# Linear attention and two MLPs on one core: six resident feature chunks instead of eight, five Strassen pairs instead of four, a fourth kv buffer, and the small elementwise work assigned anew

## The chip, the cores and the metric

The kernel runs on one core of a Trainium2 chip. The metric is the device time of one execution in microseconds. A time of a profiled execution and the span of its trace (first to last instruction) are told apart where both occur. Engines are named as in the profile: PE is TensorE (PEld its weight loads), DVE is VectorE, ACT is ScalarE, POOL is GpSimd, SP is the engine whose queue issues all loads and stores.

## The reference

Random-feature attention of 4 batches x 8 heads x 576 tokens x 64, and two MLPs (512 to 2048 to 512) on its 2304 tokens, all in fp32:

```
def phi(x):
    proj = np.einsum('bhsd,md->bhsm', x, omega)
    sq = np.sum(x * x, axis=-1, keepdims=True) / 2.0
    h = proj - sq
    h = h - np.max(h, axis=-1, keepdims=True)
    return np.exp(h) / np.sqrt(m)
q_p, k_p = (phi(q_s), phi(k_s))
kv = np.einsum('bhsm,bhsd->bhmd', k_p, v)
z = np.sum(k_p, axis=2)
num = np.einsum('bhsm,bhmd->bhsd', q_p, kv)
den = np.einsum('bhsm,bhm->bhs', q_p, z)[..., None] + 1e-06
# x = num / den, heads side by side
h = x @ w_in;  g = h * np.tanh(softplus(h));  x = g @ w_out        # first MLP (Mish)
h = x @ w_in;  g = h * sigmoid(h);            out = g @ w_out      # second MLP (SiLU)
```

## The kernel before

**Split numbers.** A matmul whose operands must keep fp32 accuracy runs as three fp32r matmuls: each operand is split into a high part (a copy rounded to fp32r, on ACT) and a low part (the rest, a subtraction). `mm3` issues high x high, low x high, high x low (lines 203 to 205).

**Attention.** There are 36 K units (batch b, unit j of 9; four heads by 128 tokens) and 36 Q units. A K unit loads `kin` (ring of 3 buffers, 5 for the first seven units), squares k (`ksqr`, one fused instruction a head on DVE, or a product on POOL with a sum on DVE and a scaling on POOL), projects (`kproj`), takes the maximum (`kmax`, DVE, L374), forms the bias in two instructions of 128x4 elements (`kba`, `kbb`, on POOL, L377 and L379), takes exp (ACT, four instructions), and adds its products with v to the batch's accumulator (`kacc`). When a batch's units of a half are done, `k_finish` leaves the split kv and the broadcast sums z in the rings `kv` and `z` (3 buffers each). A Q unit does the same up to exp (its q is split by `qhi` on ACT and `qlo` on POOL), then the denominator `den` (DVE, one fused instruction a head, or a product `fz` on POOL and a reduction on DVE), `dea`, `der` (L537, L538), the normalisation `fn`, the transpose `tr`, the split `hiT`, `loT`, and, for each second unit, the product with kv (`num`), whose result goes into the split block X by `xev` (ACT) and `xlo` (DVE, L595). Two of these, 256 tokens by 512 features, make a block; there are 9, so 18 xlo.

**First MLP beside attention (phase 0).** The weights of NA = 8 of the 16 feature chunks lie split in 16 resident tiles W. As soon as block j is there, 4 steps of two chunks each run on it: h (24 matmuls of 256 columns), Mish, the split `gh` and `gl`, and y (24 matmuls). They fill the PE between the pieces of attention. The partial results go to a scratch tensor.

**The rest (phases 1 to 4).** The other 8 chunks of the first MLP and all 16 of the second are taken in pairs by Strassen on the blocks: 512 tokens by a pair of chunks take 7 products (42 matmuls of 256 columns) and 24 matmuls of 512 columns for y; the single ninth block takes 24 and 24 of 256 columns. Phase 1 has 4 pairs for each of the 5 (double) blocks, phases 2 to 4 the 8 pairs of the second MLP, four at a time. The operands of a pair are made while the pairs before it run (`conv_pair`): load, ACT and three DVE integer instructions a weight tile (`wb`, `wo`, `ws`, lines 614 to 618), sums `sq` on DVE, and high and low parts (`sh` on ACT, `sl` on POOL, L633). They live in units of 512 columns taken from buffers that attention no longer needs: ring vw1 (34 units, 7 a pair) and vw2 (20 units, 4 a pair).

**Order.** All work is entered as tasks with an engine, a cost, a key (the due time, shifted by the table OFF) and its dependencies; `Plan.order` runs through them as a list scheduler with these costs and emits the instructions in the resulting order. Engines run their queues in that order, whatever the true times are. So the tables and costs move instructions on every engine.

Of the kernel before, what the change touches and what calls it, by code (L numbers as in the profile page):

```python
# [27 lines left out]
NA = 8  # L28
# [40 lines left out]
class Plan:  # L69
# [9 lines left out]
    def add(self, name, eng, cost, key, fn, reads=(), writes=(), new=(), after=(), lat=None, tab=None):  # L79
# [19 lines left out]
        self.tasks.append(dict(name=name, eng=eng, cost=cost, key=key, fn=fn, deps=deps, new=list(new), tab=tab,  # L99
# [94 lines left out]
def performer_two_mlps(ctx: ExitStack, tc: tile.TileContext, qin, kin, omT, w1, w2, out):  # L194
# [26 lines left out]
    ring("kv", tags("kv", 3), [P, 2, 4, 192], F32R)  # L221
    ring("z", tags("z", 3), [P, 8, NF], F32)
# [91 lines left out]
    for rg, parts in (("vw1", ((early, 11), (mid, 3), (static, 20))), ("vw2", ((early, 6), (mid, 2), (static, 12))),  # L314
# [33 lines left out]
    def sums(nm, src, sm, r, key, n, load):  # L348
# [6 lines left out]
        if VAR["sq" + nm][n] == "P":  # L355
# [646 lines left out]
```

## Time and profile before

| | |
|---|---|
| time, median of 3 runs | 989.49 us (989.46 to 990.44) |
| the profiled execution | 990.8 us |
| its span | 989.0 us |
| PE busy | 953.7 us (96%) |
| DVE busy | 616.9 us (62%) |
| ACT busy | 523.1 us (53%) |
| POOL busy | 398.7 us (40%) |
| mean granted PE clock | 0.979 of full speed |

The time is the number that the change is judged by; the span and all rows are of the one profiled execution, which is 1.3 us above the median. Matmuls are pipelined, so PE's busy time counts overlapping rows, and an interval in which it is fully busy may hold fewer matmuls than it could.

### The profile page before, as it was taken

The page shows a single profiled execution, that of the slowest core. Times are in us where ns is not written, and L with a number is a line of the kernel's source. Part 1 is how long each engine was busy: PE and PEld are TensorE (multiplying, and loading weights), DVE is VectorE, ACT ScalarE, POOL GpSimd, SP SyncE. Part 2 cuts the span into 40 slices and gives each one's busy share as a digit, 9 for nine tenths or more (in the row PEclk, how much of TensorE's full clock was granted, in tenths as well). Part 3 has the DMA queues.
Part 4 walks back from the last instruction along what each step waited for, and adds up shares of the span by engine and source line. Part 5 has one row for each costly group of instructions (what it writes and reads, how often), then busy time and mean ns, then how long its engine had stood idle before and what let it go on. Part 6 is the DMA issues. An engine that isn't in the chain of part 4 may idle for free.

```text
span 989.0 us, 17895 instructions
## 1 busy us (share of the span) xinstructions
PE 953.7 (96%) x6628; PEld 886.6 (90%) x6628; DVE 616.9 (62%) x1395; ACT 523.1 (53%) x1139; POOL 398.7 (40%) x526
## 2 busy tenths in 40 slices
PE   7888899999999999999999998999999999999998
PEld 6777799999999999898998897788988988988998
DVE  5798787648778376965543879944437864353422
ACT  4696777678878545552433465534336534334321
POOL 4788565254454255650312565704116433032100
PEclk7798899999999999999999999999999999999999
DMA  8566334322322244423232244340212301230202
GB/s 269 192 195 212 99 118 145 107 82 97 97 97 89 73 119 126 162 64 105 92 106 78 89 129 147 121 139 22 85 31 100 117 1 65 66 123 16 86 1 86
DMA packets 50360, 102.56 MB, mean 104 GB/s; under 512 B 4960, under 2 KB 17504, under 8 KB 50272
## 3 DMA queue, kind: packets, MB, share of 16 engines
q1 hardware_dynamic: 50272, 101.41, 31.8%
q8 instruction: 52, 0.85, 0.3%
q14 instruction: 36, 0.29, 0.1%
HBM read 78.85 MB, written 22.54 MB: 103 GB/s over the span
## 4 chain that ended last, share of the span: by engine, by line
PE 86%; DVE 6%; issue 2%; DMA 2%; POOL 2%; ACT 2%; SPq 0%; DVEq 0%; POOLq 0%; ACTq 0%
PE y L203 12%; PE y L204 12%; PE y L205 12%; PE h L203 5%; PE h L205 5%; PE h L204 5%; PE ha L203 4%; PE ha L204 4%; PE ha L205 4%; PE acc L422 4%; PE hb L203 3%; PE hb L204 3%; PE hb L205 3%; PE kpj L411 3%; DMA kin<-in_kin_dram 2%
## 5 line engine op out<-in xcount | busy, mean ns | idle before, releaser
L709 DVE TENSOR_TENSOR gl<-e,gh 128x512 fp32r<-128x512 f32 x144 | 109.2, 767 | 113.6 <-ACT gh L708 113.3
L205 PE MATMUL y<-gl,W 128*128 128x256 f32 (+1 forms) x528 | 170.4, 323 | 1.9 <-DVE gl L709 1.9
L203 PE MATMUL y<-gh,W 128*128 128x256 f32 (+1 forms) x528 | 171.6, 325 | 0.0
L204 PE MATMUL y<-gh,W 128*128 128x256 f32 (+1 forms) x528 | 170.3, 323 | 0.0
L708 ACT CAST gh<-e 128x512 fp32r<-128x512 f32 x144 | 88.1, 622 | 50.8 <-PE y L204 49.4
L205 PEld LDWEIGHTS y<-gl,W 128*128 128x128 f32 x528 | 99.3, 188 | 11.2 <-DVE gl L709 2.5
L203 PEld LDWEIGHTS y<-gh,W 128*128 128x128 f32 x528 | 99.5, 188 | 6.7 <-DVE stg L842 0.2
L204 PEld LDWEIGHTS y<-gh,W 128*128 128x128 f32 x528 | 99.5, 188 | 6.6
L707 ACT ACTIVATE e<-hb 128x512 f32<-128x512 f32 x48 | 28.7, 598 | 129.4 <-DVE hb L760 129.4
L633 POOL TENSOR_TENSOR LX<-Lqin,LX 128x512 fp32r<-128x512 f32 x23 | 31.7, 1380 | 137.1 <-ACT LX L632 107.0
L203 PE MATMUL h<-X,W 128*128 128x256 f32 x288 | 83.9, 291 | 0.4 <-ACT e L707 0.4
L205 PE MATMUL h<-X,W 128*128 128x256 f32 x288 | 81.7, 284 | 0.1
L204 PE MATMUL h<-X,W 128*128 128x256 f32 x288 | 81.7, 284 | 0.0
L760 DVE TENSOR_TENSOR hb<-Lfz,hb 128x256 f32<-128x256 f32 x48 | 20.5, 426 | 77.7 <-PE hb L205 77.5
L612 ACT ACTIVATE wa<-wr 128x512 f32<-128x512 f32 x64 | 42.9, 678 | 38.7 <-DVE wt L618 26.6
L633 POOL TENSOR_TENSOR LX<-Lqf,LX 128x512 fp32r<-128x512 f32 x15 | 20.7, 1385 | 101.2 <-PE ha L204 52.1
L616 DVE SCALAR_TENSOR_TENSOR wt<-wr,wt 128x512 int32<-128x512 int32 x64 | 58.3, 911 | 0.6
L411 PE MATMUL kpj<-cst,kin 128*128 128x256 f32 x144 | 45.0, 448 | 12.0 <-DMA kin<-in_kin_dram 9.7
L203 PEld LDWEIGHTS h<-X,W 128*128 128x128 f32 x288 | 55.2, 192 | 0.8 <-ACT e L707 0.6
L204 PEld LDWEIGHTS h<-X,W 128*128 128x128 f32 x288 | 55.2, 192 | 0.2
L205 PEld LDWEIGHTS h<-X,W 128*128 128x128 f32 x288 | 55.1, 191 | 0.3 <-DVE X L595 0.3
L707 ACT ACTIVATE e<-h 128x512 f32<-128x512 f32 x48 | 28.1, 598 | 47.2 <-PE h L205 47.0
(620 smaller groups left out, 3127.5 us busy)
## 6 DMA issues: line engine op xcount, KB each, us to landing
wr<-in_w_dram SPq DMA_DIRECT2D x64, 512.0 KB, 4.0
kin<-in_kin_dram SPq DMA_DIRECT2D x35, 386.0 KB, 3.5
qin<-in_qin_dram SPq DMA_DIRECT2D x36, 256.0 KB, 2.9
xf<-sx SPq DMA_DIRECT2D x18, 256.0 KB, 2.4
yp<-stg SPq DMA_DIRECT2D x18, 256.0 KB, 2.2
stg<-yp SPq DMA_DIRECT2D x18, 256.0 KB, 6.2
y<-stg SPq DMA_DIRECT2D x18, 256.0 KB, 2.3
Lqf<-y SPq DMA_DIRECT2D x18, 256.0 KB, 4.7
```

Source lines behind the costliest of these rows:

```text
L203: PE.matmul(o, s_hi, m_hi, start=first, stop=False, skip_group_check=True)
L204: PE.matmul(o, s_lo, m_hi, start=False, stop=False, skip_group_check=True)
L205: PE.matmul(o, s_hi, m_lo, start=False, stop=last, skip_group_check=True)
L411: PE.matmul(t[pj][:, jj * 256:(jj + 1) * 256], t[res][:, jj * P:(jj + 1) * P], t["cst"][:, P:P + 256], start=True, stop=True, skip_group_c ...
L422: PE.matmul(a[:, h, :], t[f][r0:r1, h * NF:(h + 1) * NF], v[r0:r1, h, :], start=first and h == 0, stop=last, skip_group_check=True)
L612: T("wm" + c, "ACT", 0.62, key, lambda: ACT.activation(t[wa], t[raw][:, :, 1].bitcast(F32), AF.Copy, scale=2.0 ** -112), reads=[raw], writ ...
L616: T("wo" + c, "DVE", 0.95, key, lambda: DVE.scalar_tensor_tensor(t[wt], t[raw][:, :, 0], 29, t[wt], ALU.logical_shift_right, ALU.bitwise_o ...
L633: T(f"sl{nm}", "Pool", 0.1 + 1.3 * n / DM, key, lambda: POOL.tensor_tensor(lo(), src(), hi().bitcast(F32), ALU.subtract), reads=res + [rh] ...
L707: T(f"X{s}.{x}", "ACT", 0.6, ks, lambda: ACT.activation(t[e], t[h], AFN), reads=res, writes=[e], new=[(e, "e")], tab=tab)
L708: T(f"gh{s}.{x}", "ACT", 0.62, ks, lambda: ACT.copy(t[gh[x]], t[e]), reads=[e], writes=[gh[x]], new=[(gh[x], "ghi")])
L709: T(f"gl{s}.{x}", "DVE", 0.69, ks, lambda: DVE.tensor_tensor(t[gl[x]], t[e], t[gh[x]].bitcast(F32), ALU.subtract), reads=[e, gh[x]], write ...
L760: T(f"{nm}{s}", "DVE", 0.43, ks, lambda: DVE.tensor_tensor(q(o, ox), q(a, ax), q(b, bx), ALU.add), reads=[r for r in (res(a, ax), res(b, b ...
```

## The change

It takes 6 instead of 8 chunks into phase 0 (3 steps a block) and makes a fifth Strassen pair of the two others. K's keys are packed closer (5 units of key a batch instead of 8) with four kv and z buffers. Nearly all K and Q squares, all bias instructions, most of qlo, all of den, most of fn and 8 of the 12 resident weights' low parts run on DVE, 8 of the 27 gl of phase 0 on POOL. The scaling by -1/16 moves into the bias instructions. Two Q units (3 and 7) project without a split. The units of vw1 and vw2 come in another order, with two fresh tiles F (35 and 20 units), and the planner's costs, keys and lead times are new, with a term that stretches DVE tasks while POOL works.

```diff
-NA = 8
+NA = 6
+NP1 = (NFC - NA) // 2
...
-QLEAD = 10.0
-KLEAD = 20.0
+QLEAD = 13.1
+KLEAD = 22.0
+KSPAN = 5
...
-VAR = dict(sqk="PDPPPPPPPPPDPPPPPPPPPPPPDPPPPPDPPPPP",
+VAR = dict(sqk="DDDDDDDDDDPDDDDDDDDDDPDDDDDDPDDDDDDD",
...
-           den="DDDDDDDDDDPPPDDDDPDPDDDPPDDPDDDDDDPP",
-           fn="AAAAPPPPDDDDPPPDDPPPPAAAAAAAAPPPPPPP",
+           den="DDDDDDDDDDDDDDDDDDDDDDDDDDDDDDDDDDDD",
+           fn="DDADDDDDDDDDDDDDDDDDDPDDDDADDDDDDDPD",
+           gl="DDPDPDDDDDDDPDDDDPPPDDDPDDPDPPPDDDPP",
+           qlo="DPPPDDDPPDDDDDPDPDDDDDDDDDDDDDDDDDPP",
+           wl="DDDPDPPPDDDDPDPD",
+           spl="SSS4SSS4SSSSSSSSSSSSSSSSSSSSSSSSSSSS")
...
+            if t["eng"] == "DVE" and t["kind"] in SHARED:
+                slow = SHARED[t["kind"]]
+                end += slow / (1 + slow) * max(0.0, min(t["cost"] * (1 + slow), free.get("Pool", 0.0) - at))
...
-    ring("kv", tags("kv", 3), [P, 2, 4, 192], F32R)
-    ring("z", tags("z", 3), [P, 8, NF], F32)
+    ring("kv", tags("kv", 4), [P, 2, 4, 192], F32R)
+    ring("z", tags("z", 4), [P, 8, NF], F32)
...
-    for rg, parts in (("vw1", ((early, 11), (mid, 3), (static, 20))), ("vw2", ((early, 6), (mid, 2), (static, 12))),
+    for rg, parts in (("vw1", ((early, 11), (fresh, 3), (mid, 5), (static, 16))), ("vw2", ((early, 6), (fresh, 1), (mid, 5), (static, 8))),
...
-                DVE.scalar_tensor_tensor(x, x, -1.0 / 16, x, ALU.mult, ALU.mult, accum_out=sm[:, r, 0, h:h + 1])
+                DVE.scalar_tensor_tensor(x, x, 1.0, x, ALU.mult, ALU.mult, accum_out=sm[:, r, 0, h:h + 1])
...
-        T(f"{nm}ba{n}", "Pool", 0.4, key, lambda: POOL.tensor_tensor(sm[:, r, 2, :], sm[:, r, 0, :], sm[:, r, 1, :], ALU.add),
+        T(f"{nm}ba{n}", "DVE", 0.09, key, lambda: DVE.scalar_tensor_tensor(sm[:, r, 2, :], sm[:, r, 0, :], -1.0 / 16, sm[:, r, 1, :], ALU.mult,
...
-        key = 8 * b + j * 8 / 9 - KLEAD
+        key = KSPAN * (b + j / 9) - KLEAD
...
-            T(f"qproj{n}", "PE", 0.72, key, proj, reads=[f"HL:{r}h", f"HL:{r}l", "om"], writes=[pj],
+            T(f"qproj{n}", "PE", 0.72, key, proj, reads=[f"HL:{r}h", f"HL:{r}l", "om"], writes=[pj], after=[f"tr{n - 3}"] if n >= 3 else [],
...
+    n1 = NP1
     for bi in (0, 1, 4, 2, 3):
-        block(1, bi, range(0, 4))
+        block(1, bi, range(0, n1))
...
-WKEY = (18.0, 25.0, 32.0, 34.0, 48.0, 64.0, 66.0, 68.0, 80.0, 98.0, 100.0, 102.0)
-XLEAD = 5.0
+W1, W2, W3 = (-20.0, -13.2, -4.4, -1.5, 1.3), (-3.4, 0.0, 1.5, 8.6), (-6.2, 0.8, 4.4, 6.5)
+XLEAD = 2.1
```

Where the order moves, two places. The first is DVE's queue early in the K work (smk holds the K units' small sums and biases, kpj a projection, kin a K unit's input, wt and W a weight on its way). Before, around the sixth projection:

```order
L357 TENSOR_REDUCE smk<-kin_245 128x4
L374 TENSOR_REDUCE smk<-kpj_279 128x4
L614 TENSOR_SCALAR wt_1_0_305<-wr_1_0_183 128x512
L449 TENSOR_TENSOR kv_135<-acc_0_216,kv_135 128x2x2x64
L616 SCALAR_TENSOR_TENSOR wt_1_0_305<-wr_1_0_183,wt_1_0_305 128x512
L357 TENSOR_REDUCE smk<-kin_261 128x4
L374 TENSOR_REDUCE smk<-kpj_315 128x4
L618 SCALAR_TENSOR_TENSOR wt_1_0_305<-wa_1_0_247,wt_1_0_305 128x512
```

And after, around the same projection:

```order
L389 TENSOR_REDUCE smk<-kpj_271 128x4
L643 TENSOR_TENSOR W_87<-wt_0_0_214,W_87 128x512
L382 SCALAR_TENSOR_TENSOR kin_267,smk<-kin_267 128x64 x4
L464 TENSOR_TENSOR kv_133<-acc_0_222,kv_133 128x2x2x64
L392 SCALAR_TENSOR_TENSOR smk<-smk 128x4
L382 SCALAR_TENSOR_TENSOR kin_281,smk<-kin_281 128x64 x4
L389 TENSOR_REDUCE smk<-kpj_305 128x4
L394 SCALAR_TENSOR_TENSOR smk<-smk 128x4
L389 TENSOR_REDUCE smk<-kpj_326 128x4
L392 SCALAR_TENSOR_TENSOR smk<-smk 128x4 x2
```

The squares (four fused rows a unit, L382), the biases (L392, L394) and the low part of a resident weight (L643) now stand in DVE's queue; the reductions of POOL's squares (L357) are gone from it.

The second is the PE's queue shortly before the fifth num (the number in kin, kpj and kf is the K unit, in acc the batch and half, in qpj and tp the Q unit, in h and y the step). Before:

```order
L205 MATMUL h5_1562<-X1_1127,W20_91 128x256
L411 MATMUL kpj25_1583<-cst_119,kin25_1371 128x256 x2
L422 MATMUL acc2_1_1337<-kin24_1329,kf24_1549 128x65 x4
L554 MATMUL tp9_1602<-cst_119,qf9_1489 128x128 x4
L203 MATMUL qpj11_1616<-om_127,HL_109 128x256
L204 MATMUL qpj11_1616<-om_127,HL_109 128x256
L205 MATMUL qpj11_1616<-om_127,HL_109 128x256
```

After:

```order
L217 MATMUL h4_1669<-X1_1087,W30_93 128x256
L437 MATMUL acc3_0_1525<-kin30_1554,kf30_1710 128x65 x4
L426 MATMUL kpj32_1744<-cst_117,kin32_1612 128x256 x2
L437 MATMUL acc3_0_1525<-kin31_1575,kf31_1734 128x65 x4
L437 MATMUL acc3_1_1764<-kin31_1575,kf31_1734 128x65 x4
L472 MATMUL zt3_0_1776<-cst_117,zb3_0_1769 128x128 x4
L215 MATMUL y0_0_1_1440<-gh2_0_1648,W41_96 128x256
```

At the same place of attention the K work has come to the units of the last batch (32 of 36), where before it was in the third (25); the Q work and the steps of phase 0 stand about where they stood.

## Rows read from the trace of the kernel before

**Rows 1.** Page, sections 1 and 2: PE's busy time, and its share in 40 slices.

```profile
PE 953.7 (96%) x6628; PEld 886.6 (90%) x6628; DVE 616.9 (62%) x1395; ACT 523.1 (53%) x1139; POOL 398.7 (40%) x526
...
PE   7888899999999999999999998999999999999998
```

**Rows 2.** Timeline of PE: start us, length, engine, line, tiles, shape, count.

```profile
179.24 1.89 PE L411 MATMUL kpj<-cst,kin 128*128 128x256 f32 x8
180.77 0.47 PE L203 MATMUL qpj<-om,HL 128*128 128x256 f32 x1
...
395.23 0.28 PE L203 MATMUL y<-gh,W 128*128 128x256 f32 x1
...
820.26 0.28 PE L203 MATMUL hb<-LX,W 128*128 128x256 f32 x1
...
823.12 0.40 PE L203 MATMUL y<-gh,Lz 128*128 128x512 f32 x1
...
825.89 0.28 PE L203 MATMUL ha<-LHL,Lkv 128*128 128x256 f32 x1
```

**Rows 3.** The first xlo (all of L595), the fifth xlo, phase 1's first matmul.

```profile
L595 DVE TENSOR_TENSOR X<-xp,X x18: 676/690/692, 63.8 to 347.0; 128x512 fp32r<-128x512 f32 x18
...
146.63 0.68 DVE L595 TENSOR_TENSOR X<-xp,X 128x512 fp32r<-128x512 f32 x1
...
396.29 0.28 PE L203 MATMUL hb<-LHL,Lkf 128*128 128x256 f32 x1
```

**Rows 4.** Windows: stretch, PE, PEld, DVE, ACT, POOL busy, PEclk, DMA, GB/s.

```profile
0.00:64.50 64.50, 51.79 (x258) 44.60 (x258) 45.53 (x131) 40.23 (x118) 43.64 (x95) 0.81 0.69 223
64.50:147.30 82.80, 73.13 (x512) 68.40 (x512) 66.48 (x199) 61.13 (x151) 56.45 (x103) 0.90 0.49 151
147.30:396.30 249.00, 246.81 (x2071) 244.89 (x2070) 169.05 (x507) 174.36 (x399) 109.85 (x173) 1.00 0.33 103
396.30:989.00 592.70, 581.96 (x3794) 528.75 (x3792) 335.81 (x561) 247.42 (x474) 188.75 (x158) 1.00 0.26 84
```

**Rows 5.** Waits, 64.5 to 147.3 us: total us, times, longest.

```profile
DVE FT L563 <- ACT FT L562: 4.2, 3, 3.1
...
SPq L405 <- PE acc L422: 31.1, 10, 11.5
```

**Rows 6.** Tiles gl and sq on DVE: length ns min/median/max, first and last start.

```profile
L709 DVE TENSOR_TENSOR gl<-e,gh x144: 674/691/1785, 108.1 to 981.5; 128x512 fp32r<-128x512 f32 x144
...
L651 DVE TENSOR_TENSOR sq<-sq,wt x12: 407/412/1499, 264.8 to 798.8; 128x256 f32<-128x256 f32 x12
```

**Rows 7.** Timeline of DVE at three places: start us, length.

```profile
137.37 0.69 DVE L374 TENSOR_REDUCE smk<-kpj 128x4 f32<-128x512 f32 x1
137.98 0.22 DVE L367 SCALAR_TENSOR_TENSOR qin<-qin 128x64 f32<-128x64 f32 x1
138.12 0.08 DVE L367 DVE_READ_ACCUMULATOR qin<-qin 128x1 f32 x1
...
160.42 0.28 DVE L529 SCALAR_TENSOR_TENSOR fz<-qf,z 128x128 f32<-128x128 f32 x1
160.63 0.08 DVE L529 DVE_READ_ACCUMULATOR fz<-qf,z 128x1 f32 x1
...
171.03 0.17 DVE L537 TENSOR_SCALAR smq<-smq 128x4 f32<-128x4 f32 x1
171.23 0.18 DVE L538 RECIPROCAL smq<-smq 128x4 f32<-128x4 f32 x1
```

**Rows 8.** Groups on POOL, 0 to 147.3 us: busy us, mean ns, idle before.

```profile
L627 POOL TENSOR_TENSOR W<-wt,W 128x512 fp32r<-128x512 f32 x16 | 21.3, 1332 | 6.9 <-ACT W L626 6.5
L356 POOL TENSOR_TENSOR kin<-kin 128x256 f32<-128x256 f32 x25 | 16.6, 664 | 8.7 <-DMA kin<-in_kin_dram 8.1 <-issue 0.2
```

**Rows 9.** Windows from 600 us on, columns as in rows 4.

```profile
600.00:625.00 25.00, 21.62 (x144) 19.40 (x143) 24.99 (x41) 13.75 (x27) 17.15 (x14) 1.00 0.43 146
...
600.00:650.00 50.00, 44.18 (x269) 38.53 (x268) 44.70 (x69) 28.90 (x58) 29.70 (x25) 1.00 0.38 126
```

More of the change, by code (lines that the diff above doesn't have):

```diff
@@ L54 @@
 TABLE = 1.3
+SHARED = dict(wb0=0.8, wo0=0.5, ws0=0.4, wl0=0.5, wb1=0.8, wo1=0.5, ws1=0.4, gl=0.5, ksqr=0.75, qsqr=0.75, den=0.75, fn=0.5,
+              qlo=0.5, xtbx=1.2, sa=1.2, kba=1.5, kbb=1.5, qba=1.5, qbb=1.5, dea=1.5)
 def kind_of(name):
@@ L98, in add @@
             self.users.setdefault(x, []).append(i)
-        self.tasks.append(dict(name=name, eng=eng, cost=cost, key=key, fn=fn, deps=deps, new=list(new), tab=tab,
+        self.tasks.append(dict(name=name, eng=eng, cost=cost, key=key, fn=fn, deps=deps, new=list(new), tab=tab, kind=kind_of(name)[0],
                                lat=LAT.get(eng, 0.0) if lat is None else lat))
@@ L532, in q_unit @@
         if den_d:
-            T(f"den{n}", "DVE", 1.7 * len(segs), key, den, reads=[f] + [f"z{b}:{g}" for b, _, _ in segs],
+            T(f"den{n}", "DVE", 0.68 * len(segs), key, den, reads=[f] + [f"z{b}:{g}" for b, _, _ in segs],
               writes=[fz, f"smq:{r}d"], new=[(fz, "fz")])
@@ L676, in performer_two_mlps @@
         for f in range(0, NA, 2):
-            steps.append(dict(ph=0, bi=j, js=[j], N=256, fs=[f, f + 1], first=f == 0, last=f == NA - 2, key=4 * j + f / 2))
+            steps.append(dict(ph=0, bi=j, js=[j], N=256, fs=[f, f + 1], first=f == 0, last=f == NA - 2, key=4 * j + 4.0 * f / NA))
     at, firsts = 4.0 * NBLK, {}
@@ L687, in block @@
             firsts["at"] += w
+    n1 = NP1
     for bi in (0, 1, 4, 2, 3):
-        block(1, bi, range(0, 4))
+        block(1, bi, range(0, n1))
     for bi in (0, 1, 4, 2):
-        block(2, bi, range(4, 8))
-    block(3, 3, range(4, 12))
+        block(2, bi, range(n1, n1 + 4))
+    block(3, 3, range(n1, n1 + 8))
     for bi in (2, 1, 0, 4):
-        block(4, bi, range(8, 12))
+        block(4, bi, range(n1 + 4, n1 + 8))
+    a0, a1, a3 = 4 * NBLK, firsts[1, 3][1], firsts[3, 3][1]
+    WKEY = [a0 + x for x in W1[:n1]] + [a1 + x for x in W2] + [a3 + x for x in W3]
     END = firsts["at"]
@@ L708, in act @@
             T(f"gh{s}.{x}", "ACT", 0.62, ks, lambda: ACT.copy(t[gh[x]], t[e]), reads=[e], writes=[gh[x]], new=[(gh[x], "ghi")])
-            T(f"gl{s}.{x}", "DVE", 0.69, ks, lambda: DVE.tensor_tensor(t[gl[x]], t[e], t[gh[x]].bitcast(F32), ALU.subtract),
+            low = "P" if ph == 0 and VAR["gl"][s] == "P" else "D"
+            T(f"gl{s}.{x}", dict(D="DVE", P="Pool")[low], dict(D=0.69, P=1.4)[low], ks, lambda: dict(D=DVE, P=POOL)[low].tensor_tensor(
+                t[gl[x]], t[e], t[gh[x]].bitcast(F32), ALU.subtract),
               reads=[e, gh[x]], writes=[gl[x]], new=[(gl[x], "glo")])
```

57 lines of the change are left out of this document (29 added, 28 removed), and 3 rows, old and new, of the table OFF.

## The prediction

> **What bounds the kernel now.** I read the page's busy times first: TensorE (PE) is busy 953.7 of 989.0 us, and its slices are below nine tenths in the first eighth, hardly elsewhere [rows 1]. A busy PE says little about its pace, so I took the pace from start to start in the timeline of two undisturbed stretches: 24 matmuls of 256 columns take 2.86 us (0.119 each), 12 of 512 take 2.77 (0.231), and nine of phase 0 take 1.06 from 395.23 to 396.29 (0.118) [rows 2, 3]. Two K units' projections take 1.53, 0.8 for one [rows 2]. Then I cut the span in four stages and asked in which of them the PE's matmuls, at that pace, fill the time. A runs to the end of the first xlo, at 64.5 us; B to the end of the fifth, at 147.3; C to the first matmul of phase 1, at 396.3; D to the end [rows 3, 4].
>
> Counting every matmul of the program's order ahead of these places at its pace (with a K unit's projection, products and transposes an estimated 2 us), the PE has 31 us of work in A, 61 in B, 245 in C and 575 in D. So A loses 33 us and B 22; C loses 4 and D 18. C and D are bound by the PE's work. A and B are not: DVE is busy 66.5 of B's 82.8 us, ACT 61.1, POOL 56.5, the granted clock is 0.90 [rows 4], and DVE's waits there are short, of nine sorts, the longest 4.2 us in all [rows 5]. Only taking PE work out, or making B shorter for the work that it does, can move the end.
>
> **The PE's work.** Nine blocks lose one pair of chunks in phase 0: 9 steps of 48 matmuls at 0.118 is 51.0 us out. A fifth pair by Strassen has, for each of four double blocks, 42 matmuls of 256 columns and 24 of 512, 5.0 + 5.54 = 10.5 us, and 48 x 0.119 = 5.7 us for the single block: 47.9 us in. Two Q units now project in four-pass fp32 instead of six split matmuls, about 0.3 us more (two of the K projections' size). Net: 2.8 us less. That is all that the PE gains; the rest is where it waits.
>
> **DVE's work, without and with GpSimd.** The old small work went partly to GpSimd, and GpSimd slows DVE. gl, which reads two SBUF tiles, has a minimum of 674 ns, a median of 691 and a maximum of 1785; sq goes from 407 to 1499 [rows 6]. Free of that, DVE's rows lie start to start 0.61 us for 512 elements, 0.146 for one head's squares (0.22 long, the accumulator's read beside the next one), 0.21 for one head of den [rows 7], that is, 0.07 to 0.08 less than their length. With those spacings I counted DVE's order ahead of the fifth xlo. Before: 93 us (38 max 23, 16 weight conversions 25, 36 sums 12, 11 den segments 9, 8 squares 5, the rest 19), and it took 147.3. After: 128 us: 48 squares of four heads at 0.585 make 28, 46 max 28, 12 conversions 18.5 and 8 low parts 5, 14 den segments 12, 92 bias rows of 128x4 at 0.09 8, 11 normalisations and 11 loT 13, 10 qlo 3, the rest 12. Ahead of the first xlo it is 39 before and 46 after. The bias rows have no row on DVE before: the nearest are L537 and L538, 0.17 and 0.18 long, 0.20 apart where one reads the other's result [rows 7]; with other work between them I take their length less 0.08, so 0.09, and keep 0.20 as the upper end.
>
> In return POOL falls nearly silent. Before, up to 147.3 us, it had 16 low parts of weights of 1.33 us, 25 K squares of 0.66 [rows 8], and the scalings, biases and products; by the new order it has 14 tensor operations ahead of the fifth num: four low parts, four qlo, five squares, one gl. I price the contention that is left in B at 3 us (2 to 4 of them collide, at the 0.7 us by which sq and gl stretch on the way to their maxima).
>
> **Stage A.** 7 us more of DVE's spacings, some 8 us less stretching, the same load order in kind (the first rows of the load queue are the K units with the same weights between them). DVE has 19 us idle here. I take no change, 64.5; bounds 62 and 69.
>
> **Stage B.** After: DVE 81 us + 3 of contention, PE 76 us (20 K projections between the first and fifth num where 11 stood). DVE is the longest. At 95% busy this is 89.5 us. I choose 95%, between B's present 80% and the 24.99 of 25 us that DVE reaches where everything waits for it [rows 9]; it is nearer to the second, because DVE is then the longest of the stage and other work stands behind each of its waits. Lower bound 82 (never idle, no contention); upper bound, B's present share of 80%: 84/0.80 = 105. So B is +6.7 us, but it holds 34 K units instead of 26 at its end.
>
> **Stage C.** The PE's work left is 286 - 107 = 179 us, where it was 336 - 92 = 245 in 249. DVE has 123 us up to the eighteenth xlo, over 155 of PE: 79%, where it was 111 over 193. The Q chain has less cover: 24 us of PE work follow the last num, 52 before. I take 7 us of loss instead of 4: C is 186. Bounds: 3 (182) and 20 (199, DVE at 85% with its stretched rows). The rule that qproj stands behind the transposes of three units earlier is an order on the PE alone, no wait. The fourth kv and z buffers cost one memset of half a microsecond on an idle POOL; without them K could not run a whole batch further ahead.
>
> **Stage D.** +47.9 for the pair. The worst stall (PE 21.6 of 25 us from 600, 44.2 of 50) comes when pairs 5 to 7 are converted while phase 2 starts: DVE 44.7 of 50 busy, POOL 29.7 [rows 9]. After, all 35 and 20 units of the weight rings are full with five pairs, so nothing is converted far ahead; but by DVE's order the 13 weights of that transition stand beside 16 gl rows instead of 10 weights beside 10. I take 2 us less: D is 638.6. Bounds 7 less (no stall left) and 8 more (pairs 2 to 4 late at the start of phase 1, or another such stall).
>
> **Sum.** 64.5 + 89.5 + 186 + 638.6 = 978.6 us of span, 10.4 less than the 989.0 of the profiled execution. That execution took 990.8 in all, the median of three runs is 989.49; the same difference gives **979 us**. Low ends together make about 960, high ends 1021.
>
> **A rule that speaks against it.** L537 and L538 show 0.17 and 0.18 us for four elements a partition [rows 7], nearly all of it fixed. [...]
>
> **Rivals.** (1) *DVE becomes the bound and the kernel is slower.* If DVE stays at B's present 80%, or a bias row holds it 0.20 us (56 of them in B, 6 us more) and it stands at 88%, B is 103 to 105; C then begins with DVE late and loses 14: 64.5 + 105 + 193 + 638.6 = 1001, **1002 us**. For it: in B all engines are tied in a web, and POOL now helps with none of it. Against: ACT and POOL hops leave the chain from the squares to exp. It decides from a busy share of DVE below 84% in B, where B is 100 and the gain is gone. (2) *K's buffers set the pace: no change.* kin has three buffers, and the loads already wait 31.1 us in B for the products that free them [rows 5]. 20 K units in 89.5 us leave 13.4 us for load, squares, max, bias, exp and product; the present B takes 3 x 7.5 = 22. At 15 us B is 100, and the time **989 us**: the change only moved K's work. Against: K units waited there because their keys were spread, not because a chain needs 22 us. (3) *More than forecast.* DVE at 98%, C losing 3, D's stall at 600 gone: 63 + 86 + 182 + 635 = 966, **966 us**. For it: the old stretch of gl and wt by GpSimd goes from all of A to C.
>
> **How the numbers follow.** Forecast (970 to 987) 0.44; rival 3 0.20; rival 2 0.13; rival 1 0.23. Two tenths of a per cent, 2 us, is about what a measurement of this kernel can tell from no change. Faster 0.64, same 0.13, slower 0.23. The range reaches to rival 3's middle and near to rival 1's: 964 to 998; the forecast's own is 970 to 987.
>
> **What would show it.** Right: the fifth xlo near 154 us with 34 K units done; DVE over 90% busy between 65 and 154; gl's median and mean alike up to phase 1; PE full from 154 to a first phase 1 matmul near 340; D 638 us. Wrong: the fifth xlo after 165, idle DVE there behind ACT or loads, PE gaps over 15 us between the fifth xlo and phase 1, or new PE waits for pairs 2 to 4 or 5 to 8 in phases 1 and 2.

## The result and the profile after

The changed kernel takes **1004.1 us** (median of four, 999.1 to 1004.7) where the kernel before takes 990.0 beside it: a ratio of 1.0136, 95% interval 1.0105 to 1.0168. Measured again later (e9 below) it was 998.2 (997.1 to 1003.4), ratio 1.0110 (1.0066 to 1.0154). It is 1.1 to 1.4% slower; the prediction was 979 and faster. The profiled execution took 1004.05 us with a span of 1002.3. Executions of this kernel differ by some 6 us even where nothing is changed, and the last section shows where; A and B of one profile are read with that margin. D differs too: it is 651.8 in this profile, and 649.6, 650.7 and 647.8 in three more runs with the same order of work from there on (e9, e2, e1).

The page of the profile after: busy time, and PE's share in 40 slices (cf. [rows 1]).

```profile
PE 962.8 (96%) x6504; PEld 889.5 (89%) x6504; DVE 678.8 (68%) x1989; ACT 516.7 (52%) x1106; POOL 270.8 (27%) x241
...
PE   8877899999999989999999999899999999999998
```

The four stages by windows, as in [rows 4]; they end at the first and fifth xlo and at phase 1's first matmul.

```profile
0.00:65.00 65.00, 54.74 (x253) 46.67 (x254) 48.98 (x280) 34.55 (x102) 6.33 (x14) 0.76 0.62 204
65.00:169.00 104.00, 90.41 (x624) 84.78 (x623) 86.70 (x479) 70.90 (x185) 10.51 (x11) 0.92 0.41 128
169.00:350.50 181.50, 179.90 (x1527) 178.98 (x1526) 160.82 (x618) 137.86 (x302) 45.87 (x43) 1.00 0.36 116
350.50:1002.30 651.80, 637.80 (x4106) 579.06 (x4104) 382.32 (x616) 273.38 (x518) 208.04 (x174) 0.99 0.26 84
```

I counted the PE's rows of each stage at the pace of [rows 2] (0.117 us for 256 columns, 0.232 for 512, 0.216 for each row of a K projection, 0.11 for the small ones). A stage's length less this work is its loss, in us:

| stage | before | forecast | after | loss before | loss after |
|---|---|---|---|---|---|
| A | 64.5 | 64.5 | 65.0 | 29.5 | 30.3 |
| B | 82.8 | 89.5 | 104.0 | 19.5 | 24.3 |
| C | 249.0 | 186 | 181.5 | 5.8 | 4.6 |
| D | 592.7 | 638.6 | 651.8 | 16.6 | 28.1 |

PE's work itself went from 917.65 to 914.97 us, 2.7 less (forecast 2.8 less). So the change lost 16 us: 11.5 in D and 5.6 in A and B, and gained 1.2 in C. B and D are the two steps to explain.

B: what SP and DVE wait for (cf. [rows 5]; total us, times, longest). The K loads now wait 57 us for the products that free the three kin buffers, where it was 31.

```profile
SPq L420 <- PE acc L437: 57.0, 18, 9.2
...
DVE smk L389 <- PE kpj L426: 7.2, 7, 3.0
```

D: the two stretches that hold 17 of its 28 us of loss by the same count. The second lost 7 us before ([rows 9]: PE 44.2 of 50) and loses 9.5 now; the start of phase 1 lost 2 before and loses 8.

```profile
350.00:375.00 25.00, 20.89 (x142) 20.21 (x142) 23.93 (x31) 13.30 (x28) 18.73 (x16) 0.86 0.56 179
...
600.00:650.00 50.00, 44.64 (x262) 39.91 (x262) 42.78 (x65) 24.84 (x47) 25.65 (x22) 0.93 0.30 96
```

DVE hardly rests there, and POOL is busy beside it. What the PE waits for after 345 us is above all DVE (total us, times, longest):

```profile
PE ha L215 <- DVE hb L781: 8.9, 5, 2.7
PE ha L215 <- ACT e L726: 1.8, 1, 1.8
```

The granted clock adds to it. Before, it was 1.00 in all of D [rows 4]; now it is 0.86 and 0.93 in the two stretches above. A mean of 0.86 over 25 us and of 0.93 over 50 says that the PE stood at the lower of its two levels for some 14 us in all, which costs up to 7 us where it had work: an estimate from these two rows. (Windows of 1 us show 1.00 or 0.50, but for those in which the level changes; matmuls of 256 columns begin 0.21 us apart at 356 us, at 0.50, and 0.12 at 351, at 1.00.) In this trace each of the four falls comes within 2 us of the end of a PE gap of 1.8 to 2.7 us. Not every such gap brings one: before, the clock stayed up behind a gap of 3.1 us at 612.

The timeline of DVE and POOL at the start of phase 1, DVE first (start, length):

```profile
349.80 1.67 DVE L633 SCALAR_TENSOR_TENSOR wt<-wa,wt 128x512 int32<-128x512 int32 x1
351.39 1.76 DVE L729 TENSOR_TENSOR gl<-e,gh 128x512 fp32r<-128x512 f32 x1
353.07 1.50 DVE L629 TENSOR_SCALAR wt<-wr 128x512 int32<-128x512 int32 x1
354.61 1.66 DVE L631 SCALAR_TENSOR_TENSOR wt<-wr,wt 128x512 int32<-128x512 int32 x1
356.30 0.69 DVE L633 SCALAR_TENSOR_TENSOR wt<-wa,wt 128x512 int32<-128x512 int32 x1
...
349.18 1.74 POOL L649 TENSOR_TENSOR LHL<-wt,LHL 128x512 fp32r<-128x512 f32 x1
350.88 1.73 POOL L649 TENSOR_TENSOR LX<-Lqin,LX 128x512 fp32r<-128x512 f32 x1
352.75 1.55 POOL L649 TENSOR_TENSOR LHL<-wt,LHL 128x512 fp32r<-128x512 f32 x1
354.25 1.47 POOL L649 TENSOR_TENSOR LX<-Lqin,LX 128x512 fp32r<-128x512 f32 x1
```

The two engines take turns. POOL's first row ends at 350.92, DVE's at 351.47; POOL's second at 352.61, DVE's at 353.15; and so on. A DVE row that takes 0.69 us by itself takes 1.7 when it begins beside a POOL row, and only the last one, with POOL idle, has its own length. POOL's rows are stretched too (the shortest of this kind in the trace take 1.27). L649 is the subtraction that makes the low parts of the pairs' weights and of the inputs. The gl that DVE does in phase 0, on the other hand, are free of this now (length in ns, minimum, median and maximum up to 350 us; the maximum over all was 1785 in [rows 6]):

```profile
L729 DVE TENSOR_TENSOR gl<-e,gh x18: 660/682/693, 127.8 to 343.9; 128x512 fp32r<-128x512 f32 x18
```

### The profile page after: what moved, and what is told of

The parts are those of the page before. It is cut to its first block, busy times and chain, and to the rows that moved or that the text cites. A ratio compares the mean times of both kernels' runs of the same rounds, so it can differ in the third digit from the quotient of the medians.

```text
span 1002.3 us, 17826 instructions
## 1 busy us (share of the span) xinstructions
PE 962.8 (96%) x6504; PEld 889.5 (89%) x6504; DVE 678.8 (68%) x1989; ACT 516.7 (52%) x1106; POOL 270.8 (27%) x241
## 4 chain that ended last, share of the span: by engine, by line
PE 59%; DVE 4%; POOL 2%; issue 1%; ACT 0%; DVEq 0%; POOLq 0%; ACTq 0%
PE y L215 10%; PE y L216 10%; PE y L217 10%; PE ha L215 5%; PE ha L216 5%; PE ha L217 5%; PE hb L216 4%; PE hb L215 3%; PE hb L217 3%; PE h L217 1%; PE h L216 1%; PE h L215 1%; DVE wt L629 1%; DVE gl L729 1%; POOL W L649 1%
## 5 line engine op out<-in xcount | busy, mean ns | idle before, releaser
L729 DVE TENSOR_TENSOR gl<-e,gh 128x512 fp32r<-128x512 f32 x136 | 105.4, 782 | 151.7 <-ACT gh L727 143.9
L215 PE MATMUL y<-gh,W 128*128 128x256 f32 (+1 forms) x376 | 122.8, 326 | 0.0
L216 PE MATMUL y<-gh,W 128*128 128x256 f32 (+1 forms) x376 | 121.3, 323 | 0.0
L217 PE MATMUL y<-gl,W 128*128 128x256 f32 (+1 forms) x376 | 121.1, 322 | 0.0
L217 PEld LDWEIGHTS y<-gl,W 128*128 128x128 f32 x376 | 71.7, 191 | 5.8
L215 PEld LDWEIGHTS y<-gh,W 128*128 128x128 f32 x376 | 72.1, 192 | 4.3
L216 PEld LDWEIGHTS y<-gh,W 128*128 128x128 f32 x376 | 72.1, 192 | 4.2
L215 PE MATMUL h<-X,W 128*128 128x256 f32 x216 | 62.6, 290 | 0.0
L216 PE MATMUL h<-X,W 128*128 128x256 f32 x216 | 60.7, 281 | 0.0
L217 PE MATMUL h<-X,W 128*128 128x256 f32 x216 | 60.7, 281 | 0.0
L631 DVE SCALAR_TENSOR_TENSOR wt<-wr,wt 128x512 int32<-128x512 int32 x64 | 60.0, 938 | 0.4
L437 PEld LDWEIGHTS acc<-kin,kf 128*128 128x128 f32 (+1 forms) x320 | 49.0, 242 | 11.0 <-ACT kf L399 9.3
L437 PE MATMUL acc<-kin,kf 128*128 128x65 f32 (+1 forms) x320 | 50.4, 327 | 7.4 <-ACT kf L399 7.4
L781 DVE TENSOR_TENSOR Lfz<-Lfz,ha 128x256 f32<-128x256 f32 x52 | 21.7, 418 | 50.2 <-PE ha L217 47.9
L633 DVE SCALAR_TENSOR_TENSOR wt<-wa,wt 128x512 int32<-128x512 int32 x64 | 54.0, 849 | 0.4
L649 POOL TENSOR_TENSOR LX<-Lqin,LX 128x512 fp32r<-128x512 f32 x23 | 33.2, 1449 | 64.5 <-ACT LX L648 33.2
L629 DVE TENSOR_SCALAR wt<-wr 128x512 int32<-128x512 int32 x64 | 44.6, 699 | 4.9 <-POOL LFT L649 1.5
```

What stands on the lines that cost most here:

```text
L215: PE.matmul(o, s_hi, m_hi, start=first, stop=False, skip_group_check=True)
L216: PE.matmul(o, s_lo, m_hi, start=False, stop=False, skip_group_check=True)
L217: PE.matmul(o, s_hi, m_lo, start=False, stop=last, skip_group_check=True)
L437: PE.matmul(a[:, h, :], t[f][r0:r1, h * NF:(h + 1) * NF], v[r0:r1, h, :], start=first and h == 0, stop=last, skip_group_check=True)
L629: T("wb" + c, "DVE", 0.43, key, lambda: DVE.tensor_scalar(t[wt], t[raw][:, :, 1], -0x80000000, None, ALU.bitwise_and), reads=[raw], writes ...
L631: T("wo" + c, "DVE", 0.68, key, lambda: DVE.scalar_tensor_tensor(t[wt], t[raw][:, :, 0], 29, t[wt], ALU.logical_shift_right, ALU.bitwise_o ...
```

## The experiments

In the texts below, theory 1 is for B that the three kin buffers set its pace, and for D that POOL's reads and DVE stretch each other; theory 2 is for B that DVE's work sets it. Times are medians; ratios are to the kernel before, run beside each. A+B (to the fifth xlo), C and D are of the one profiled execution, which can lie some us off the median: that of e5 (985.0) is the shortest of ten, that of e6 (998.1) is 4.6 us longer than its median.

| run | time | ratio (95%) | A+B | C | D |
|---|---|---|---|---|---|
| e1_kin4 | 998.8 | 1.0086 (1.0057 to 1.0115) | 166.0 | 181.9 | 647.8 |
| e2_max32 | 993.4 | 1.0039 (1.0019 to 1.0059) | 157.6 | 181.3 | 650.7 |
| e3_slmem | 979.4 | 0.9913 (0.9883 to 0.9944) | 161.9 | 179.2 | 634.9 |
| e4_before_small | 993.6 | 1.0037 (1.0012 to 1.0062) | 155.4 | 248.5 | 589.5 |
| e5_sldve | 988.8 | 0.9996 (0.9970 to 1.0022) | 161.6 | 184.8 | 636.8 |
| e6_before_sldve | 993.5 | 1.0045 (1.0014 to 1.0076) | 146.5 | 248.8 | 601.0 |
| e7_oldsmall | 1013.7 | 1.0230 (1.0196 to 1.0263) | 150.3 | 213.3 | 647.8 |
| e8_sldve_kin4 | 989.1 | 0.9980 (0.9952 to 1.0007) | 164.5 | 184.8 | 635.3 |
| e9_after_again | 998.2 | 1.0110 (1.0066 to 1.0154) | 170.6 | 181.5 | 649.6 |
| e10_actsquares | 1006.0 | 1.0180 (1.0143 to 1.0216) | 158.8 | 208.6 | 637.4 |
| e11_kspread | 1015.7 | 1.0272 (1.0221 to 1.0323) | 137.7 | 239.2 | 637.3 |
| e12_twice_projected | 994.1 | 1.0059 (1.0037 to 1.0081) | 168.8 | 185.9 | 636.9 |
| e13_pairs01_pool | 991.6 | 1.0014 (0.9992 to 1.0035) | 168.0 | 181.5 | 640.8 |
| e14_actsquares_fixed | 987.8 | 0.9982 (0.9955 to 1.0009) | 163.1 | 184.4 | 636.9 |
| e15_both | 982.9 | 0.9927 (0.9898 to 0.9956) | 159.9 | 185.5 | 636.8 |
| e16_before_slmem | 981.2 | 0.9913 (0.9885 to 0.9941) | 145.5 | 249.0 | 584.7 |
| e17_before_sldve_fixed | 985.4 | 0.9966 (0.9942 to 0.9989) | 147.2 | 248.9 | 587.8 |
| e18_sldve_fixed_actsq | 979.2 | 0.9904 (0.9873 to 0.9935) | 164.5 | 179.6 | 634.6 |

### D: POOL's reads beside DVE

**e3_slmem**, in `split`:

```
+        def low():
+            for _ in range(2):
+                POOL.memset(lo().bitcast(F32), 0.0)
+            POOL.tensor_tensor(lo()[:, 0:16], src()[:, 0:16], hi()[:, 0:16].bitcast(F32), ALU.subtract)
...
-        T(f"sl{nm}", "Pool", 0.1 + 1.3 * n / DM, key, lambda: POOL.tensor_tensor(lo(), src(), hi()...
+        T(f"sl{nm}", "Pool", 0.1 + 1.3 * n / DM, key, low,
```

> The changed kernel, but in the pairs' and inputs' splits GpSimd subtracts 16 columns only and fills the low part with zeros twice, which reads no SBUF (this leaves out nearly all of the low parts); same order, GpSimd about as long. Theory 1 (D lost 11 us because DVE and GpSimd stretch each other where pairs 2 to 4 are converted at the start of phase 1): wt, sq and gl fall back to 0.43 to 0.69 us there, PE's loss between 350 and 375 goes from 7.9 to under 3, D from 651.8 to about 643, the time to about 995. Theory 2 (the conversions are late since their space comes free late, however fast the engines are): D stays above 649, the time above 1001.

D fell by 16.9 us, twice what theory 1 asked, and the time by 19 to 25. Two stretches of this kernel, and the first of them in the changed kernel:

```profile
375.00:600.00 225.00, 224.21 (x1466) 204.10 (x1465) 113.31 (x220) 93.58 (x176) 70.64 (x179) 1.00 0.29 94
600.00:650.00 50.00, 50.00 (x316) 45.06 (x315) 26.95 (x54) 25.59 (x50) 17.59 (x46) 1.00 0.28 90
```

```profile
375.00:600.00 225.00, 224.94 (x1468) 204.39 (x1467) 133.59 (x218) 91.72 (x176) 72.93 (x61) 1.00 0.26 85
```

From 375 to 600 POOL is as busy as in the changed kernel (70.6 us, there 72.9), and DVE's busy time is 113.3 where it is 133.6. The DVE groups from 350 us on, of the changed kernel (D begins 9 us earlier in e3, so fewer rows are counted there):

```profile
L631 DVE SCALAR_TENSOR_TENSOR wt<-wr,wt 128x512 int32<-128x512 int32 x40 | 41.3, 1034 | 0.3
...
L629 DVE TENSOR_SCALAR wt<-wr 128x512 int32<-128x512 int32 x40 | 31.5, 789 | 3.7 <-POOL Lz L649 1.2 <-POOL W L649 1.1 <-POOL Lzb L649 0.6
L781 DVE TENSOR_TENSOR hb<-Lfz,hb 128x256 f32<-128x256 f32 x52 | 22.2, 427 | 22.9 <-PE hb L217 22.5
```

and the same operations in e3 (busy, mean ns):

```profile
L631 DVE SCALAR_TENSOR_TENSOR wt<-wr,wt 128x512 int32<-128x512 int32 x37 | 25.2, 684 | 0.2
...
L786 DVE TENSOR_TENSOR hb<-Lfz,hb 128x256 f32<-128x256 f32 x52 | 22.2, 428 | 29.1 <-PE hb L217 28.9
...
L629 DVE TENSOR_SCALAR wt<-wr 128x512 int32<-128x512 int32 x37 | 19.9, 539 | 3.9 <-POOL LFT L651 2.3 <-POOL Lkv L651 0.8 <-POOL W L651 0.5
```

The PE waits for the sums hardly at all any more:

```profile
PE ha L215 <- DVE hb L786: 1.3, 2, 0.8
PE ha L215 <- ACT e L731: 0.4, 1, 0.4
```

So it is POOL's reading of SBUF, not its busy time; the sums that take one operand from PSUM (hb) never felt it, but they stand in DVE's queue behind rows that did. D is 634.9, under the forecast, and the clock is 1.00 in it. The 16.9 us are made up of 9 us of PE waits (10.7 in the changed kernel, 1.7 here) and up to 7 us of lower clock. Since D of the unchanged order was 647.8 to 651.8, the price is 13 to 17 us.

**e16_before_slmem**, the same edit in the kernel before.

> The kernel before with GpSimd's splits replaced as in the third run: 16 columns subtracted, the rest of the low parts filled with zeros twice (this leaves out nearly all of the low parts), order kept. If the same contention made the stalls of D before (7 us from 600, 2 from 400): D 582 to 585 instead of 592.7, PE full from 600 to 650, the time 979 to 983; the changed kernel's 17 us then hold 8 to 10 that were there already. If those stalls were late conversions: D 589 to 594, the time 986 to 991.

D is 584.7, 8.0 us less, and PE is busy 48.9 of 50 us from 600:

```profile
600.00:650.00 50.00, 48.85 (x300) 43.50 (x299) 34.41 (x70) 27.40 (x55) 25.82 (x64) 1.00 0.42 131
```

The stall of [rows 9] was this all along; the forecast had put it down to the conversions themselves. The changed kernel holds 16.9 us of it against 8.0, 9 us more, of which some 7 are the lower clock. With it gone from both, 979.4 stands against 981.2, and both ratios are 0.9913: within the 0.3% of the intervals the two are level, so of the 10 us that the forecast had the change gain little is seen.

**e5_sldve** and **e6_before_sldve**: the subtraction on DVE, planned anew.

```
-        T(f"sl{nm}", "Pool", 0.1 + 1.3 * n / DM, key, lambda: POOL.tensor_tensor(lo(), src(), ...
+        T(f"sl{nm}", "DVE", 0.08 + 0.6 * n / DM, key, lambda: DVE.tensor_tensor(lo(), src(), ...
```

> The changed kernel with the low parts of the pairs' and inputs' splits subtracted on DVE instead of GpSimd, planned anew with DVE's cost; nothing is left out. Theory 1 (in D GpSimd's SBUF reads and DVE stretch each other): gl, wt and sq keep to 0.42 to 0.69 us, DVE is busy 36 to 42 of the 50 us from 600, PE full there and from 350 to 375, D 635 to 641, the time 980 to 987. Rival (these splits are simply too much work at the pair changes, and on one engine they take longer): D 645 to 655, the time 997 to 1006.

D is 636.8, as theory 1 said, with nothing left out; from 600 to 650 (second window of e5) DVE does all of it and PE is never idle:

```profile
600.00:650.00 50.00, 50.00 (x314) 44.81 (x313) 37.81 (x78) 25.95 (x51) 0.00 (x0) 1.00 0.26 87
```

The median, 988.8, is 2 us over the range given; C came out 3 us longer.

> The same move of the splits' low parts to DVE in the kernel before, nothing else. Theory 1: the PE loses 7 us between 600 and 650 and 2 after 400 to the same contention; without it D goes from 592.7 to 582 to 586, A to C as before, the time to 979 to 984. Rival (the old stalls are late conversions or old small work): D 590 to 594, the time 988 to 993.

The D of both readings missed: it is 601.0. The contention is gone, but the new order put a pair's conversion back to back in DVE's queue ahead of the sums that the PE waits for:

```profile
PE ha L203 <- DVE hb L760: 7.2, 1, 7.2
PE y L203 <- DVE stg L842: 2.7, 1, 2.7
```

**e17_before_sldve_fixed**: the same work on DVE, but in the places of the kernel's own order (the planner keeps POOL's cost).

> The kernel before with the splits' low parts on DVE in its own order (where planned anew it had a new stall of 15 us at 600); nothing is left out. If that stall came from the new order: D 583 to 588, the time 980 to 985, under both kernels. If DVE cannot take them at the pair changes: D 592 to 602, the time 989 to 999.

D 587.8, the time 985.4: the order had made the stall of e6. **e13_pairs01_pool** leaves the two pairs that are converted beside attention on POOL.

> The changed kernel with the splits' low parts on DVE, but those of pairs 0 and 1, which are converted beside attention, on GpSimd; nothing is left out. If C's 5.6 us of PE loss at 250 with all of them on DVE comes from these: C 181 to 182 instead of 184.8, D 636 to 639, the time 984 to 987, under 988.8. If their contention costs as much as their time on DVE: 987 to 991.

C was 181.5 as expected, but D was 640.8, in yet another order, and the time of 991.6 is above both ranges.

### B: buffers, DVE, clock

**e1_kin4**, and **e8_sldve_kin4** on top of e5:

```
+                if ring in ("kin0", "kin"):
+                    tag = ("kin0", "kin1", "kin2", "X0", "X1")[loads] if loads < 5 else f"kin{(loads - 2) % 4}"
+                    loads += 1
```

> The changed kernel with a fourth buffer for the K inputs and nothing else: every engine's order stays as it is. Theory 1 (the three kin buffers set B's pace: 20 K units in 104 us are 5.2 each, 15.6 a buffer): four buffers allow 3.9 a unit, B then goes to PE's and DVE's work, 94 to 97 us instead of 104, loads wait under 25 us there instead of 57, and the time is about 996. Theory 2 (DVE's own work and the turns between DVE, PE and ACT set it): the loads wait less, B stays at 102 to 104 and the time at 1002 to 1004.

> The first kernel of this group with the fourth kin buffer at the same order; nothing is left out. If the buffers are worth what the fourth one gained alone (1004 to 999): 3 to 6 us under the first of this group, B 99 to 101, loads waiting under 30 us there, 976 to 983. If that was a difference of executions: within 2 us of it.

In e1 the loads wait a third of what they did (57.0):

```profile
SPq L424 <- PE acc L441: 17.9, 10, 4.6
```

but B is 100.4, inside the margin and far from the 94 to 97 of theory 1, and e8 lies 0.3 us from e5. So the waiting of the loads did not set B's length. Theory 1 falls for B, and with it the prediction's rival 2.

**e9_after_again**: no edit.

> The changed kernel once more, beside the others of this group on their chip: 1000 to 1005 if the fourth kin buffer's 5 us were real, 997 to 1000 if they lay between executions and chips.

998.2: e1's gain lay between executions.

**e2_max32**, and **e15_both** with e5's edit as well:

```
-        ... DVE.tensor_reduce(sm[:, r, 1, :], v(), AX.X, ALU.max)
+        ... DVE.tensor_reduce(sm[:, r, 1, :], v()[:, :, 0:32], AX.X, ALU.max)
```

> The changed kernel with the maximum over the first 32 of a head's 128 projections instead of all (this leaves out part of the computation), same order, three kin buffers: takes some 0.4 us of DVE out of each of 72 K and Q units, about 13 us in B, and shortens a K unit's own chain by the same 0.4. Theory 1 (buffers): a turn goes from 15.6 to about 15.2, B to 101, the time to about 1001. Theory 2 (DVE's work): B falls by 9 to 13 us to 91 to 95, A by 3 to 6, and the time to 988 to 992.

> The changed kernel with both suspected costs cut: the splits' low parts on DVE, and the maximum over 32 of 128 projections (this leaves out part of the computation), in the order of the first alone. If the two steps that failed are DVE's share in A and B and GpSimd's reads in D, and add up: A and B 153 to 158, D 636 to 638, the time 976 to 981, the predicted one. If something else is short too: 983 or more.

e2 looked like theory 2: the fifth xlo 11.4 us earlier. But e3, whose queues are the changed kernel's up to 218 us, has it 7.1 us earlier too. Against e5 the shorter maximum (e15) gives 1.7 us at the fifth xlo, though DVE's busy time in B falls by 9.7. A and B together are 159.9, not the 153 to 158 of the case that the two steps add up. B in e5 and in e15:

```profile
61.40:161.60 100.20, 87.96 (x619) 82.40 (x618) 86.67 (x478) 70.68 (x184) 10.61 (x11) 0.91 0.45 136
```

```profile
60.10:159.90 99.80, 89.01 (x619) 83.88 (x618) 76.98 (x479) 70.75 (x184) 10.74 (x11) 0.91 0.44 138
```

The medians differ by more, 0.9927 against 0.9996, some 7 us for 28 us of DVE work (72 maxima of 0.29 instead of 0.68); e5's profile is of its shortest execution, so the 1.7 is read too low. Over all profiles with this K order but e12, B is 97.7 to 99.8 with 76 to 77 us of DVE work in it (e2, e15) and 99.9 to 105.4 with 83 to 88. So DVE's work counts for something, about a quarter of its length, and does not set B.

**e10_actsquares** (planned anew) and **e14_actsquares_fixed** (e5's order):

```
+                if nm == "k" and n < 30 and n % 2:
+                    ACT.activation(x, x, AF.Square, accum_out=sm[:, r, 0, h:h + 1])
```

> The changed kernel with the splits' low parts on DVE, and the squares of every second K unit up to the thirtieth on ACT (four squarings with a sum each) instead of DVE; nothing is left out. Takes 15 x 0.585 = 8.8 us off DVE in A and B, puts 15 x 1.2 = 18 on ACT, which is idle 30 us in A and 33 in B. Theory 2 (DVE's work sets A and B; the shorter maximum gave 11 us for 19): A and B together 4 to 6 us shorter, the time 982 to 985. Rival (the turns between engines set them, and an ACT hop lengthens the turn): A and B the same or up to 8 longer, the time 988 to 996.

> The changed kernel with the splits' low parts on DVE, in that kernel's order, but the squares of every second K unit up to the thirtieth issued on ACT in the place that they had; nothing is left out. Theory 2 (DVE's work sets A and B): 8.8 us less of it give 3 to 6 us, A and B together 157 to 161, and the time 983 to 986; the 18 us longer time of the version planned anew was its order. Rival (a turn through ACT is longer, whatever the order): A and B 165 to 175, the time 992 to 1005.

e10's new plan spread its cost over C (208.6) and told nothing of B. e14 gains 1.0 us of 988.8, less than the intervals; A and B together are 163.1. It shows neither theory 2's 3 to 6 us nor the rival's longer turn.

**e12_twice_projected**:

```
-            for jj in range(2):
+            for jj in (0, 1) * (2 if n < 24 else 1):
```

> The changed kernel with the splits' low parts on DVE, and the first 24 K units' projections computed twice into the same bank, same order; nothing is left out, 24 x 0.43 us or more of PE work is added. If the low granted clock (0.76 up to the first xlo, 0.75 to 0.83 up to 106 us) sets A and early B: the clock rises there above 0.85, A and B shrink by 3 to 8 us, the time 981 to 986. If DVE's work sets them: A and B within 3 us, 987 to 992. If the PE is tied in the turn: 5 to 10 longer, 994 to 999.

The granted clock rose (0.97 in B below), yet B is 103.4 long: its 9 us of extra PE work ate what the clock gave. The loss of B fell from 21.6 us (e5) to 16.1, so the clock holds a part of it. A and B together are 7 us longer and the time is 994.1, as the third reading had it.

```profile
65.40:168.80 103.40, 93.08 (x659) 86.52 (x658) 86.73 (x479) 70.59 (x184) 10.37 (x11) 0.97 0.41 132
```

### The other parts of the change

**e4_before_small** (the small work moved in the kernel before, eight chunks), **e7_oldsmall** (all of the change but that) and **e11_kspread** (e5 with `key = 8 * (b + j / 9) - 20.0` for K):

> The kernel before with the small work alone moved as in the change (squares, bias rows, den, normalisation, some low parts of q, weights and gl), with the new cost figures and offsets of the planner; still eight resident chunks, four pairs, three kv buffers and the old lead of K and Q. If the small work on DVE is what made A and B long: A above 66, B above 86, the time 993 to 998 against 990 before. If it is K's closer spacing on three buffers and the fifth pair that cost, and the small work gains what its contention was: B 78 to 82, C 1 to 2 us less, D as before within 3 us, the time 983 to 988.

> The changed kernel (six resident chunks, five pairs, four kv buffers, the new lead and offsets) with the small work where the kernel before had it, on GpSimd for much of squares, biases, den and low parts. Theory 2 (DVE's work sets A and B): taking 30 us of DVE off makes B 88 to 97, gl's mean in C goes to 0.85 us or more and C to 183 to 188, the time 993 to 1003. Theory 1 for B (K's closer spacing on three kin buffers): B stays at 102 to 108, the time 1003 to 1012.

> The changed kernel with the splits' low parts on DVE, and K's units spread over eight steps a batch with the old lead of 20 instead of five with 22; nothing is left out. If moving K forward is what made B long without giving it back: B 82 to 90, C 196 to 202, A to C 2 to 8 us shorter, the time 980 to 986. If K's work only moves (DVE has the same work up to the last num): A to C within 3 us of 346, the time 986 to 991. If C has too little cover for it: A to C 5 or more longer, 994 and more.

With eight chunks the move costs 3.4 us: B grows by 8 and C, covered by the PE's work, gives nothing back (D gains 3). With six chunks it gains 9 to 12 us by the ratios: without it (e7) B is 20 us shorter, but C 32 longer, and the time is above both ranges. K's closer spacing is worth 27 us (e11 against e5, each in a plan of its own): undone, B is 81 and C 239, the third reading, with A to C 30 us longer. The C of e7 and e11:

```profile
150.30:363.60 213.30, 201.45 (x1635) 197.10 (x1634) 162.83 (x480) 145.01 (x342) 99.14 (x142) 0.97 0.35 109
```

```profile
137.70:376.90 239.20, 220.65 (x1758) 215.73 (x1757) 185.78 (x811) 165.10 (x382) 15.12 (x15) 0.96 0.39 121
```

So both parts are needed with six chunks, and B and C can't be judged apart: what leaves one turns up in the other.

### A version that beats both

**e18_sldve_fixed_actsq**: the changed kernel in its own order, the splits' low parts on DVE and every second K unit's squares on ACT.

> The changed kernel in its own order throughout, with the splits' low parts issued on DVE and every second K unit's squares up to the thirtieth on ACT; nothing is left out. If the order planned anew is not what took the contention away: C 180 to 183, D 635 to 640, the time 981 to 987. If DVE, in an order made for shorter work, falls behind at the pair changes: D 642 to 650, the time 990 to 998.

979.2 us, 1.0% under the kernel before (0.9904, 0.9873 to 0.9935), with nothing left out. The kernel before with the same move of the splits, run beside it (e17), is at 0.9966, so the change, with the squares moved to ACT, adds 0.6%. The order is the changed kernel's own, so it is the move to DVE, and not a new plan, that takes D from 651.8 to 634.6. Its C and D:

```profile
164.50:344.10 179.60, 179.31 (x1527) 178.84 (x1526) 158.97 (x654) 139.18 (x305) 12.64 (x12) 1.00 0.39 121
344.10:978.80 634.70, 630.30 (x4106) 573.33 (x4105) 388.61 (x784) 270.82 (x515) 1.51 (x1) 1.00 0.27 85
```

## Why the prediction was wrong

**D, the step that failed.** "I take 2 us less" was 11 more: 651.8 against 638.6, beyond the upper bound of 648.6. I had read POOL's and DVE's busy shares beside the stall of [rows 9], and had gl's and sq's maxima in [rows 6], yet priced contention in A and B only, where the change takes POOL's work away; the lower clock that a stall can bring stood in D at nothing. In D the change takes none away and adds a pair: the twelve weights of pairs 2 to 4 are converted between 321 and 389 us (the wt rows of DVE's timeline), with the first inputs of phase 1 among them. e3, e5, e18 and e16 show the price: 13 to 17 us after, 8.0 before. Without it D was 634.6 to 636.8, and 634.9 against 584.7 (e3, e16) is 50.2, so the 47.9 for the pair was nearly right. Of the 8 us that the start of phase 1 loses now, some 3.5 are the lower clock (0.86 over 25 us). Why the PE has gaps there that it had not before, with twelve weights in 72 us there too, is not settled by a run of its own.

**B, the second.** "At 95% busy this is 89.5 us" failed (84 us at 95% are 88.4; 89.5 takes 85): it was 104.0 (100.2 in e5). DVE's work was sized well (86.7 busy), its share was 83%, and that is below the 84% from which rival 1 was to decide. But e15 shows that DVE's work is not what sets B. What held is simpler: the PE's work in B plus the loss that the stage had before. The loss is 19.5 us before and 19 to 26 in every run with the changed kernel's K order but e12 (16), where the forecast had 13.5; with the PE's work (79.7 counted, forecast 76) this makes 99 to 105. A part of the loss is the granted clock: 0.92 over 104.0 us means about 17 us at half speed, so up to 8 us, and as much before (0.90 over 82.8). The forecast named the 0.90 and gave it no term. Less buffers waiting and less DVE work did not take the rest away; what its chain is stays open.

**A, C and the PE's net** held: 65.0 for 64.5, 181.5 for 186 (just under its low bound of 182), 2.7 us less for 2.8. The contention in A to C vanished but for the splits of pairs 0 to 2 in C, which was the gain argued for. The bias rows were priced rightly: they begin 0.08 to 0.12 us apart in the changed kernel (timeline of DVE), so all 144 cost about 13 us. The two Q projections without a split are four rows of 256 columns each in the trace (L515), where the split ones are six; at 0.216 and 0.117 us a row that is 0.16 us more for each, as priced.

```profile
112.07 0.15 DVE L392 SCALAR_TENSOR_TENSOR smq<-smq 128x4 f32<-128x4 f32 x1
112.19 0.16 DVE L392 SCALAR_TENSOR_TENSOR smk<-smk 128x4 f32<-128x4 f32 x1
112.27 0.15 DVE L394 SCALAR_TENSOR_TENSOR smq<-smq 128x4 f32<-128x4 f32 x1
112.38 0.16 DVE L394 SCALAR_TENSOR_TENSOR smk<-smk 128x4 f32<-128x4 f32 x1
```

**The rivals.** Rival 1 gave 1002 us, near the result, but for another reason: B's 105 was there, its C (193) was not, and D was not its subject. Rival 2's buffers are excluded by e1 and e8. Rival 3's D (635) came true only without POOL's reads (634.6 to 635.3 in e3, e8 and e18). And e3's 979.4 agrees with the forecast partly by chance: its B is 10 us longer and its C 7 and D 4 shorter than forecast.

## What to carry to other kernels

Where DVE and POOL both read SBUF, add their times: a stretch whose DVE rows at free length and POOL rows together fill it can stall whoever waits for DVE, even if each alone looks loose. (This is an estimate from the two stretches that follow.) From 600 to 650 us here DVE's 27.0 (e3) and POOL's 25.7 make 52.6 of 50, and the PE lost 9.5; from 375 to 600 the 113.3 and 72.9 make 186 of 225, and it was never idle. Price a stall with the clock that it may bring down: here the lower clock cost up to 7 us beside 11 of waits. In B a wait in a stage that no engine fills added to the work put there; it did not shrink because the busiest engine had room. And after work is moved to another engine, compare the new plan with the same work in the old order: the same edit in two orders differed here by 8 to 18 us (e17 and e6, e18 and e14, e14 and e10; the first two pairs by 0.8% in their ratios).

## What the runs showed of the hardware

**Turns on SBUF.** In the changed kernel 51 rows of DVE with two inputs in SBUF (gl of L729, wt of L631 and L633; 0.68 to 0.69 us by themselves) began under a POOL row that reads SBUF and took over 0.9 us. From the 5th to the 95th percentile they end 0.545 to 0.552 us after that POOL row's end, however early they began under it; read from these ends, DVE waits for the whole of the POOL row and then does its own work. In e3, where POOL mostly fills memory, such rows keep to their length: from 350 us on their means are 0.684 (L631), 0.686 (L633) and 0.692 us (gl), where the changed kernel has 1.034, 0.901 and 0.801. Rows that read one operand from PSUM are not delayed (hb, 0.43 in both). The wt rows of L629, with one input, are 0.42 us by themselves and took 0.95 in the median under POOL's reading rows; in e3 their mean is 0.539, so something delays them there too, and whether it is the fills or the subtractions of 16 columns is not shown.

**The clock between executions.** Up to 218 us the changed kernel, its repetition (e9) and e3 issue the same instructions, yet the fifth xlo ends at 169.0, 170.6 and 161.9. They part between 50 and 90 us, where the granted clock, a mean over its two levels, differs at the same busy time of the PE. The changed kernel, then e3:

```profile
50.00:90.00 40.00, 31.12 (x150) 28.58 (x151) 31.49 (x186) 21.33 (x63) 2.54 (x2) 0.73 0.40 126
```

```profile
50.00:90.00 40.00, 31.91 (x191) 29.04 (x190) 34.10 (x208) 24.44 (x74) 3.83 (x3) 0.85 0.52 164
```

150 matmuls in one, 191 in the other. Why one execution gets the lower clock there, the runs don't show.
